# The fourth batch's attention beside the third batch's FFN, and weights narrowed in five operations: attention with sinks and a channel MLP on one core

## The chip, the cores and the metric

The kernel runs on one core of a Trainium2 chip, as one launch. The time is the device time of an execution in microseconds (us). Engines are called TensorE (PE, with its weight loads as PEld), VectorE (DVE), ScalarE (ACT), GpSimd (POOL) and SyncE (SP), whose queue issues nearly all DMAs.

## The reference

```python
scores = scale * np.matmul(q, k.transpose(0, 1, 3, 2))      # 4 batches, 8 heads, S 768, D 64
keep = is_sink | in_window                                  # 4 sink keys, a window of 128
scores = np.where(keep, scores, -1000000000.0)
scores = scores - np.max(scores, axis=-1, keepdims=True)
a = np.exp(scores)
a = a / (np.sum(a, axis=-1, keepdims=True) + 1e-09)
attn = np.matmul(a, v)
...
x = attn.transpose(0, 2, 1, 3).reshape(B, S, H * D)         # 768 x 512 for each batch
xt = x.transpose(0, 2, 1)
h = xt @ U @ V                                              # U 768 x 32, V 32 x 768
u = x + h.transpose(0, 2, 1)
ch = np.maximum(u @ w_ch1, 0.0) @ w_ch2                     # 512 -> 2048 -> 512
return u + ch
```

## The kernel before

Each batch goes through three stages: attention in pairs of heads, the mixing over the sequence (rank 32), and the FFN with its residual. The FFN is most of TensorE's work, so the vector work of one batch's attention is laid beside the FFN of another batch. The table `AHEAD` says which: for the FFN of batch b, the batches that are attended to meanwhile, each with the step at which it begins and a distance:

```python
AHEAD = {0: ((1, 3, 2),), 1: ((2, 0, 1.5), (3, 12, 1.5)), 2: (), 3: ()}
```

All steps are first handed to a planner (class `Plan`), each with its engine or a choice of engines with a cost, what it reads and writes, and a due time. The planner lays them out by its own costs (`order`, with passes backward and forward), tries changes of its due times drawn from numbers that `SEED` and the table `MOVES` fix (`nudge`), and settles for each engine the sequence of its instructions, that of SyncE's DMAs included. Instructions are then issued in that sequence. A change of a cost or of one of these numbers can thus reorder the whole program.

Attention of a pair of heads and half of the rows (`attend`): scores on TensorE (L798), mask and maximum on VectorE (L807, L812), exponentials on ScalarE (L816), the sum plus 1e-9 (L823, on ScalarE or VectorE) and its reciprocal (L826), scaling on ScalarE in three pieces (L834) or GpSimd in one (L837), the copy of the sink columns (L842 to L844), transposes (L857), masked copies `oph` and `opf` (L862, L659), values (L889). K and q are put into two buffers each, `kp` and `qp`, by SyncE's queue (L674), where a load waits until the matmuls of the pair two before have read its buffer.

Mixing: `mix_start` loads the values of the sinks (`vsr`) and splits them into a rounded part and a low part `vsh` (L660, L666, L668), `mix_half` and `mix_end` compute the product with U on TensorE (L1019, L1020), its rounded form `t` (L659 and, for the low part, L1059), the product with V (L1071, L1072) and the sum with x in `xT` (L1074). The function `tt` takes VectorE or GpSimd (L666, L668), `copy` takes ScalarE or VectorE (L659, L660).

Weights, U and V arrive as 64-bit floats. `narrow` turns each piece of up to 512 columns into 32-bit floats on the chip with the steps of `join_steps`: L152 or L153 takes the upper 16 bits, L154 the middle ones, L155 clamps them, L156 or L157 moves the exponent, L158 puts the sign back, L159 (VectorE) or L160 (GpSimd) joins both halves. Weights are then split into a rounded part (cast, L659) and a low part (L666, L668). The one FFN that runs while weights are still arriving is batch 0's (`ffn`): first layer L1109 to L1111 on `uh` and `ul`, the rounded and the low part of u, then `hh` and `hl` (L1117, L1120), and second layer L1131.

Batches 1 to 3 use `ffn_joint`, which forms seven products where eight blocks would be (L1279) from sums of weights `ws` and differences `wd` that lie in DRAM by then; each 256 KB piece is loaded by SyncE's queue and read by six matmuls of 128x384. `combine` forms the sums of u. For batch 2, u lies in DRAM and `combine` reloads it into the buffers `kp` and `qp` (the branch `if b == 2`). This is open to it because `AHEAD` has both batch 2 and batch 3 attended to beside the FFN of batch 1: once that is done, `kp` and `qp` are free. The FFNs of batches 2 and 3 have no attention beside them. After batch 1's FFN, more SBUF is given to weight pieces (`widen`), 13 buffers instead of 7.

## Time and profile before

| | us |
|---|---|
| median of 3 runs | 664.59 |
| the runs | 664.59, 661.3, 665.56 |
| the profiled execution | 662.35 |
| its span | 660.6 |
| TensorE busy | 642.9 |
| VectorE busy | 517.1 |
| ScalarE busy | 436.0 |
| GpSimd busy | 223.1 |

The span runs from the first to the last instruction of the profiled execution. The batches' FFNs follow one another: first matmul of batch 0's at 59.22 us, of batch 1's at 227.97, of batch 2's at 412.01, of batch 3's near 537. Pure matmuls of 128x384 start 0.175 us apart, though each is shown with a length of about 0.33.

### The profile page before, as it was taken

The numbers are of one execution on the slowest core, as the hardware profiler recorded it, in microseconds if no ns is written. First come the engines' busy times: TensorE is split into PE (matmuls) and PEld (weight loads), VectorE is DVE, ScalarE is ACT, GpSimd is POOL, SyncE is SP. The second block draws the span as 40 slices with busy tenths as digits, with TensorE's granted clock in tenths as the row PEclk, the third lists the DMA queues.
The fourth block names the chain that finished last, engine by engine and source line by source line (L and its number), as shares of the span: only waits on it lengthen the run. The fifth ranks groups of instructions, "written<-read, shape, count | busy, mean of one in ns | idle before, by whom it ended". The sixth has DMA issues, their size and how long they took to land.

```text
span 660.6 us, 15908 instructions
## 1 busy us (share of the span) xinstructions
PE 642.9 (97%) x5526; PEld 599.7 (91%) x5526; DVE 517.1 (78%) x1472; ACT 436.0 (66%) x1201; POOL 223.1 (34%) x244
## 2 busy tenths in 40 slices
PE   7899999999999999999999999999999999999996
...
GB/s 254 219 226 382 354 391 350 360 322 352 304 271 336 271 345 377 339 311 215 321 307 360 220 239 287 288 302 250 235 258 247 281 327 342 250 246 247 252 270 92
DMA packets 111721, 191.60 MB, mean 290 GB/s; under 512 B 10256, under 2 KB 46608, under 8 KB 111632
## 3 DMA queue, kind: packets, MB, share of 16 engines
...
q14 instruction: 43, 0.35, 0.2%
...
## 4 chain that ended last, share of the span: by engine, by line
PE 86%; DVE 8%; DMA 3%; issue 1%; POOL 1%; ACT 0%; SPq 0%; DVEq 0%; ACTq 0%; POOLq 0%
PE bank L1279 51%; PE bank L1131 10%; PE bank L798 4%; PE bank L889 4%; PE bank L1109 3%; PE bank L1111 3%; PE bank L1110 3%; PE bank L857 3%; DMA ws<-spare 1%; DVE p L812 1%; DVE w L666 1%; DMA qp<-in_q_dram 1%; DVE spare L666 1%; PE bank L979 1%; DMA kp<-in_k_dram 1%
## 5 line engine op out<-in xcount | busy, mean ns | idle before, releaser
L1279 PE MATMUL bank<-w,w 128*128 128x384 f32 x792 | 155.1, 339 | 0.0
L1279 PEld LDWEIGHTS bank<-w,w 128*128 128x128 f32 x792 | 138.6, 188 | 2.1 <-issue 1.2
L816 ACT ACTIVATE p<-p,mn 128x132 f32<-128x132 f32 x192 | 75.4, 395 | 8.3 <-DVE mn L812 8.1
L1279 PE MATMUL bank<-w,spare 128*128 128x384 f32 x348 | 68.4, 338 | 0.5 <-DVE w L666 0.5
L668 POOL TENSOR_TENSOR spare<-spare 128x128 f32<-128x128 f32 (+1 forms) x56 | 46.2, 837 | 61.6 <-ACT spare L659 13.1
L1284 DVE TENSOR_TENSOR big<-bank,big 128x384 f32<-128x384 f32 x84 | 44.7, 551 | 23.1 <-PE bank L1279 22.8
L1279 PEld LDWEIGHTS bank<-w,spare 128*128 128x128 f32 x348 | 61.6, 188 | 1.0 <-DVE w L666 0.9
L1131 PE MATMUL bank<-w,hh 128*128 128x512 f32 x192 | 61.3, 400 | 0.0
L668 POOL TENSOR_TENSOR w<-uh,w 128x384 fp32r<-128x384 f32 x17 | 17.4, 1021 | 90.9 <-ACT w L659 78.5
L812 DVE CUSTOM_DVE_ANT_0 p<-bank,mask 128x132 f32<-128x132 f32 x192 | 47.5, 291 | 0.2
L659 ACT CAST w<-ul 128x384 fp32r<-128x384 f32 x57 | 29.3, 514 | 23.0 <-PE bank L1279 21.2
L1109 PE MATMUL bank<-ul,w 128*128 128x384 f32 x128 | 43.9, 343 | 0.6 <-POOL ul L668 0.6
L1111 PE MATMUL bank<-uh,w 128*128 128x384 f32 x128 | 43.1, 337 | 0.0
L1110 PE MATMUL bank<-uh,w 128*128 128x384 f32 x128 | 43.0, 336 | 0.0
L1279 PE MATMUL bank<-spare,w 128*128 128x384 f32 x210 | 42.9, 340 | 0.0
L798 PE MATMUL bank<-kp,qp 64*64 64x198 f32 (+3 forms) x840 | 40.7, 325 | 1.4 <-DMA kp<-in_k_dram 1.4
L1131 PEld LDWEIGHTS bank<-w,hh 128*128 128x128 f32 x192 | 34.7, 188 | 6.6 <-issue 1.9
L666 DVE TENSOR_TENSOR w<-ul,w 128x384 fp32r<-128x384 f32 x50 | 30.4, 615 | 10.8 <-ACT w L659 10.4
L1279 PEld LDWEIGHTS bank<-spare,w 128*128 128x128 f32 x210 | 37.0, 188 | 1.4 <-DVE mn L812 0.3
L1131 PE MATMUL bank<-w,hl 128*128 128x512 f32 x96 | 37.9, 395 | 0.0
L834 ACT ACTIVATE p<-p,r 128x132 f32<-128x132 f32 x114 | 36.8, 395 | 0.5 <-DVE r L826 0.5
L798 PEld LDWEIGHTS bank<-kp,qp 64*64 64x64 f32 x840 | 28.9, 139 | 8.6 <-issue 5.3
...
## 6 DMA issues: line engine op xcount, KB each, us to landing
w<-ws SPq DMA_DIRECT2D x132, 256.0 KB, 4.3
w<-wd SPq DMA_DIRECT2D x102, 256.0 KB, 4.2
...
spare<-ws SPq DMA_DIRECT2D x60, 256.0 KB, 3.9
...
spare<-wd SPq DMA_DIRECT2D x42, 256.0 KB, 3.8
...
```

Of the source, the lines that this page charges most:

```text
L666: ways = {"DVE": (dve(n), lambda: nc.vector.tensor_tensor(dst(), a(), b(), op), pool)}
L668: ways["POOL"] = (gps(n), lambda: nc.gpsimd.tensor_tensor(dst(), a(), b(), op), True)
L798: nc.tensor.matmul(st()[a * G:(a + 1) * G, x * TW + to:x * TW + to + wd], qr()[at, q0:q0 + G], kr()[at, k0:k0 + wd], start=True, stop=True ...
L812: add("DVE", dve(SW), lambda st=st, i=i, j=j, at0=x * TW + base + 2 * i, part=part, at=at: nc.vector.tensor_tensor_reduce(part().rearrange ...
L816: add("ACT", act(SW) + 0.22, lambda part=part, at=at: nc.scalar.activation(part(), part(), AF.Exp, bias=at(mn), scale=-1.0, accum_out=at(sm)),
L834: nc.scalar.activation(p()[:, u, i], p()[:, u, i], AF.Copy, scale=r()[:, i * NBLK + u:i * NBLK + u + 1])
L1109: nc.tensor.matmul(ph()[:, :CH], wh, ul()[:, c, :], start=n == 0, stop=False)
L1110: nc.tensor.matmul(ph()[:, :CH], wl, uh()[:, c, :], start=False, stop=False)
L1111: nc.tensor.matmul(ph()[:, :CH], wh, uh()[:, c, :], start=False, stop=n == NC - 1)
L1131: nc.tensor.matmul(acc[k](), a()[:, sl], w()[:, :, at, m:m + P].rearrange("p d o j -> p o d j"), start=not begin and i == 0 and j == 0, st ...
L1279: nc.tensor.matmul(bank()[:, :CH], w()[:, at:at + P], u()[:, d, :] if n > 1 else u(), start=first and i == 1, stop=last and i == 3 * n, sk ...
L1284: add("DVE", dve(CH), lambda: nc.vector.tensor_tensor(x(), bank()[:, :CH], t(), ALU.add), r=(bank,) if t is x else (bank, t), w=(x,), prio ...
```

## The change

The attention of batch 3 is laid beside the FFN of batch 2, and `combine` reads batch 2's sums from the tiles in which they were formed, without the way through DRAM into `kp` and `qp`.

`join_steps` has five steps in place of six. The clamp goes; its lower end is in the shift of the exponent (a Relu of ScalarE with a bias of −8·14336 in a tile `low`, or two instructions of VectorE), its upper end in a minimum of the step that adds (L172). The sign is put in by the last step (L173). Both last steps are VectorE's alone: GpSimd narrows nothing.

GpSimd may take three more kinds of steps: the sink copies and the copies of U into `uf`, and the sum plus 1e-9. The low part of the sinks' values is formed on 32 rows instead of 64, the fourth copy of these values is zero, and the sinks' factor is 1/3 instead of 1/4. For the very first rows of the first pair, the first score step covers one tile of 128 rows and the second two, where it was two and one. The second part of the first k is loaded by ScalarE's queue, behind q; the masks are filled ahead of reading a flag. Costs of the planner for transposes, values and one copy change, and so do SEED and the table MOVES (202 numbers, before 75; cut below).

```diff
@@ -58,25 +58,36 @@
 PRICE = {"DVE": 3.0, "ACT": 1.5, "POOL": 1.5}
-SEED = 510000000
+SEED = 820000000
 SHARES = ((0.02, 6), (0.1, 3), (0.5, 1), (0.005, 15))
...
 MOVES = (
-    14, 17, 59, 72, 119, 122, 174, 241, 268, 327, 385, 575, 576, 601, 647, 662, 670, 673, 700, 759,
...
+    38, 41, 43, 85, 93, 158, 277, 294, 310, 348, 382, 413, 874, 985, 1231, 1234, 1276, 1539, 1665,
...
 )
...
 NEARLY = 1
-VALUES = 2.1
+VALUES = 2.0
 JOINT = (1, 2, 3)
...
 SCRATCH = 1024
-AHEAD = {0: ((1, 3, 2),), 1: ((2, 0, 1.5), (3, 12, 1.5)), 2: (), 3: ()}
+AHEAD = {0: ((1, 3, 2),), 1: ((2, 0, 1.5),), 2: ((3, 0, 1.5),), 3: ()}
 NSLOT = 3
@@ -100,6 +111,7 @@
 TOP_MIN = struct.unpack("f", struct.pack("I", 0x38100000))[0]
+HIGH = float(0x7F80)
 TOP_MAX = struct.unpack("f", struct.pack("I", 0x47EF0000))[0]
@@ -138,7 +150,7 @@
-def join_steps(nc, raw, n, a, t, out):
+def join_steps(nc, raw, n, a, t, out, low):
@@ -146,18 +158,19 @@
     ab = lambda: a().bitcast(BF16)
-    high = lambda: t().bitcast(U16)[:, 1:2 * n:2]
+    high = lambda: f32(t())[:, :n]
     v = nc.vector
+
+    def shifted():
+        v.tensor_scalar(a(), a(), 14336.0, 0.0, ALU.subtract, ALU.max)
+        v.tensor_scalar(high(), a(), 8.0, None, ALU.mult)
     return [
...
         {"ACT": lambda: nc.scalar.activation(x(), mid(), AF.Copy, scale=2.0 ** -13)},
-        {"DVE": lambda: v.tensor_scalar(ab(), ab(), TOP_MIN, TOP_MAX, ALU.max, ALU.min)},
-        {"DVE": lambda: v.tensor_scalar(a(), a(), 14336.0, 8.0, ALU.subtract, ALU.mult),
-          "ACT": lambda: nc.scalar.activation(a(), a(), AF.Copy, bias=-114688.0, scale=8.0)},
-        {"DVE": lambda: v.scalar_tensor_tensor(high(), top(), 0x8000, a(), ALU.bitwise_and, ALU.bitwise_or)},
-        {"DVE": lambda: v.tensor_tensor(x16(), high(), x16(), ALU.add),
-         "POOL": lambda: nc.gpsimd.tensor_tensor(x(), words(t())[:, :n], x(), ALU.add)},
+        {"ACT": lambda: nc.scalar.activation(high(), a(), AF.Relu, bias=low, scale=8.0), "DVE": shifted},
+        {"DVE": lambda: v.scalar_tensor_tensor(x16(), high(), HIGH, x16(), ALU.min, ALU.add)},
+        {"DVE": lambda: v.scalar_tensor_tensor(x16(), top(), 0x8000, x16(), ALU.bitwise_and, ALU.bitwise_or)},
     ]
@@ -653,12 +666,14 @@
-    def copy(self, n, dst, src, psum=False, **kw):
+    def copy(self, n, dst, src, psum=False, pool=False, **kw):
...
         nc = self.nc
-        return self.plan.any({"ACT": (act(n) + (0.0 if psum else 0.045), lambda: nc.scalar.copy(dst(), src()), False),
-                       "DVE": (dve(n) if psum else dve2(n), lambda: nc.vector.tensor_copy(dst(), src()), not psum)},
-                      **kw)
+        ways = {"ACT": (act(n) + (0.0 if psum else 0.045), lambda: nc.scalar.copy(dst(), src()), False),
+                "DVE": (dve(n) if psum else dve2(n), lambda: nc.vector.tensor_copy(dst(), src()), not psum)}
+        if pool:
+            ways["POOL"] = (0.13 + n * 1.1e-3, lambda: nc.gpsimd.tensor_copy(dst(), src()), True)
+        return self.plan.any(ways, **kw)
@@ -688,9 +703,9 @@
         held = (self.held,) if self.raws_seen > NHELD else ()
-        steps = join_steps(self.nc, raw, n, lambda: A()[:, :n], T, flat)
-        use = (((top,), A), ((mid,), flat) if flat else ((), mid), ((), A), ((), A), ((top, A), T), ((T,), flat or mid))
-        cost = (0.069 + n * 0.52e-3, 0.0, 0.069 + n * 0.26e-3, 0.069 + n * 0.26e-3, 0.05 + dve(n), dve(n))
+        steps = join_steps(self.nc, raw, n, lambda: A()[:, :n], T, flat, self.low)
+        use = (((top,), A), ((mid,), flat) if flat else ((), mid), ((A,), T), ((T,), flat or mid), ((top,), flat or mid))
+        cost = (0.069 + n * 0.52e-3, 0.0, 0.138 + n * 0.78e-3, 0.05 + dve(n), 0.05 + dve(n))
         for ways, (r, w), c in zip(steps, use, cost):
@@ -708,9 +723,9 @@
         add("POOL", 0.3, lambda: nc.gpsimd.memset(uf()[:, :, RANK:2 * RANK], 0.0), w=((uf, 1),), prio=pr)
-        self.copy(n, lambda: uf()[:, :, 0:RANK], uv, r=(ub,), w=((uf, 0),), prio=pr)
+        self.copy(n, lambda: uf()[:, :, 0:RANK], uv, pool=True, r=(ub,), w=((uf, 0),), prio=pr)
         self.copy(2 * n, lambda: uf()[:, :, 2 * RANK:].rearrange("p n (a r) -> p n a r", a=2),
-                  lambda: uv().unsqueeze(2).broadcast_to([P, NB, 2, RANK]), r=(ub,), w=((uf, 2),), prio=pr)
+                  lambda: uv().unsqueeze(2).broadcast_to([P, NB, 2, RANK]), pool=True, r=(ub,), w=((uf, 2),), prio=pr)
         for c in range(S // VC):
@@ -821,6 +836,7 @@
         self.plan.any({"ACT": (0.2, lambda: nc.scalar.activation(r(), sm(), AF.Copy, bias=1e-9)),
+                       "POOL": (0.17, lambda: nc.gpsimd.tensor_scalar(r(), sm(), 1e-9, None, ALU.add), True),
                        "DVE": (0.4, lambda: nc.vector.scalar_tensor_tensor(
@@ -855,7 +871,7 @@
                     nc.tensor.transpose(tr()[:, u * P:(u + 1) * P], p().rearrange("p u i w -> p u (i w)")[:, u, at:at + 2 * P - 1:2], self.ident)
-            add("PE", 0.30, mms, r=parts + [box], w=(tr,), prio=t0)
+            add("PE", 0.33, mms, r=parts + [box], w=(tr,), prio=t0)
             banks.append(tr)
@@ -895,12 +911,12 @@
                 src = to if part == 0 else slice(D - to.start, D - to.start + D)
-                self.copy(CH, lambda to=to, cols=cols, xT=xT: xT()[to, cols], lambda src=src, part=part: banks[part]()[src, :CH],
+                self.copy(CH + 85 * part, lambda to=to, cols=cols, xT=xT: xT()[to, cols], lambda src=src, part=part: banks[part]()[src, :CH],
                           psum=True, r=(banks[part],), w=((xT, half),), prio=t0)
...
         row = p, _, sm = self.p(), self.mn(), self.sm()
-        for js in TILES:
+        for js in TILES if b or half or pair else ((0,), (1, 2)):
             self.scores(half, js, t0, q, kr, row)
@@ -939,12 +955,9 @@
-        def vlow(g):
-            sl = slice(g * 32, g * 32 + 32)
-            self.tt(DM, lambda: vs()[sl], lambda: vsr()[sl], lambda: f32(vs()[sl]), ALU.subtract,
-                    r=(vsr,), w=(vs,), prio=t0 - 8)
-        vlow(1)
-        vlow(3)
+        sl = slice(0, 32)
+        self.tt(DM, lambda: vs()[sl], lambda: vsr()[sl], lambda: f32(vs()[sl]), ALU.subtract,
+                r=(vsr,), w=(vs,), prio=t0 - 8)
         self.mixing[b] = vs, None, self.bank
@@ -958,7 +971,7 @@
         self.copy(CH, four, lambda: psink()[:, hs].rearrange("p n h c -> p n (h c)").unsqueeze(2).broadcast_to(
-            [P, NBLK, 4, 32]), r=(psink,), w=(rep,), prio=t0)
+            [P, NBLK, 4, 32]), pool=True, r=(psink,), w=(rep,), prio=t0)
         tr = self.bank()
@@ -1034,7 +1047,7 @@
         part = self.pst(lambda t: f32(t)[:, :P])
-        add("DVE", dve(P), lambda: nc.vector.tensor_scalar(part(), by()[:, :P], 0.25, None, ALU.mult),
+        add("DVE", dve(P), lambda: nc.vector.tensor_scalar(part(), by()[:, :P], 1.0 / 3.0, None, ALU.mult),
             r=(by,), w=(part,), prio=t0)
@@ -1228,13 +1241,6 @@
         xs = self.x[b]
-        if b == 2:
-            us, xs = self.over([((g.boxes[i::NRAW - 1][-1],), lambda g=g, i=i: g.boxes[i::NRAW - 1][-1]()[:, :S])
-                                for g in (self.kp, self.qp) for i in range(NRAW - 1)]), []
-            for d in range(NC):
-                x, ud = us(), self.ud[b][d]
-                self.put(x, lambda x=x, ud=ud: (x(), ud()), 393216, t0, r=(ud,))
-                xs.append(x)
         hi, lo = zip(*[(self.uc(), self.uc()) for _ in range(7)])
@@ -1700,9 +1706,12 @@
                 pre.tile([P, n], F32, name=f"{x}{h}") for x, n in (("kp", NB * SW), ("qp", S))]
-            for part in (slice(0, 2 * SW), slice(2 * SW, NB * SW)):
-                nc.sync.dma_start(kt[:, part], k[0, h][:, part])
-            nc.scalar.dma_start(qt[:, :CH], q[0, h][:, :CH])
+            if h == 0:
+                nc.scalar.dma_start(qt[:, :CH], q[0, h][:, :CH])
+            for x, part in enumerate((slice(0, 2 * SW), slice(2 * SW, NB * SW))):
+                (nc.scalar if h == 0 and x else nc.sync).dma_start(kt[:, part], k[0, h][:, part])
+            if h:
+                nc.scalar.dma_start(qt[:, :CH], q[0, h][:, :CH])
         kept["vp", 0] = pre.tile([P, 2 * NB, D], F32, name="vp0")
@@ -1715,18 +1724,20 @@
         nc.gpsimd.memset(tri, 1.0)
+        low = sp.tile([P, 1], F32, name="low")
+        nc.gpsimd.memset(low, -8.0 * 14336.0)
         for at in (slice(0, G), slice(G, P)):
...
         ns, w, flag = values()
+        masks.fill(ns, w)
         rv = nc.values_load(flag[0:1, 0:1], min_val=0, max_val=1)
-        masks.fill(ns, w)
         nc.gpsimd.memset(join, 0)
...
         with ExitStack() as fctx:
-            Fast(tc, fctx, masks.m, (masks.now, masks.past), tri, ident, kept, pairs, bigs, join,
+            Fast(tc, fctx, masks.m, (masks.now, masks.past), tri, low, ident, kept, pairs, bigs, join,
                  q, k, v, vs, U, V, w1, w2, out).run()
@@ -1763,6 +1774,7 @@
         vs[:, :, h, :, h // 2, h % 2, :] = v[:, None, h, [0, 2, 1, 3] if h % 2 else [2, 0, 3, 1], :]
+    vs[:, 3] = 0.0
     u, vv, w1, w2 = (a["moe_" + n] for n in ("U", "V", "w_ch1", "w_ch2"))
```

What this does to the sequence of instructions is seen at three places.

ScalarE, ahead of the second layer of batch 0's FFN: `uh` are rounded parts of x, `w1_979` (before) and `w1_1073` (after) the first weight of the second layer, `spare0` its narrowed form (of before lines L153, L154, L659; of after L169 to L171, L672). Before:

```order
L659 CAST uh0_1015<-xT1_470 128x384
L659 CAST uh1_1023<-xT1_470 128x384
L153 ACTIVATE nr_1030<-big0_101 128x512
L659 CAST uh1_1023<-xT3_673 128x384
L659 CAST uh1_1023<-xT4_670 128x384
L659 CAST uh1_1023<-xT2_474 128x384
L659 CAST uh0_1015<-xT2_474 128x384
L659 CAST uh0_1015<-xT3_673 128x384
L659 CAST uh0_1015<-xT4_670 128x384
L659 CAST w1_979<-spare0_189 128x4x128
```

After:

```order
L169 ACTIVATE nr_1032<-big2_104 128x512
L672 CAST uh0_989<-xT4_646 128x384
L170 ACTIVATE spare0_191<-big2_104 128x512
L171 ACTIVATE nt_106<-nr_1032,low_127 128x512
L169 ACTIVATE nr_1047<-big3_105 128x512
L170 ACTIVATE spare1_192<-big3_105 128x512
L1130 ACTIVATE hh0_1059<-bank0_183 128x384
L171 ACTIVATE nt_106<-nr_1047,low_127 128x512
L169 ACTIVATE nr_1069<-big0_101 128x512
L672 CAST w1_1073<-spare0_191 128x4x128
L171 ACTIVATE nt_106<-nr_1069,low_127 128x512
L672 CAST w1_1073<-spare0_191 128x4x128
```

The passes over the second half of the first weight (`big2`) stand in the row behind the casts of x that are left, where before both halves had been passed over earlier and only the last cast of this weight is behind them.

VectorE, the same place: the last additions to `xT`, the low parts `ul`, the low part of that weight and the first `hl`. Before:

```order
L1074 TENSOR_TENSOR xT3_673<-xT3_673,bank6_187 128x384
L1074 TENSOR_TENSOR xT4_670<-xT4_670,bank1_182 128x384
L666 TENSOR_TENSOR ul1_1041<-xT2_474,uh1_1023 128x384
L666 TENSOR_TENSOR ul1_1041<-xT4_670,uh1_1023 128x384
L666 TENSOR_TENSOR ul0_1028<-xT2_474,uh0_1015 128x384
L666 TENSOR_TENSOR ul0_1028<-xT3_673,uh0_1015 128x384
L666 TENSOR_TENSOR ul0_1028<-xT4_670,uh0_1015 128x384
L666 TENSOR_TENSOR w1_979<-spare0_189,w1_979 128x4x128
L1120 SCALAR_TENSOR_TENSOR hl0_1092<-bank5_186,hh0_1083 128x384
```

After:

```order
L1087 TENSOR_TENSOR xT4_646<-xT4_646,bank5_188 128x384
L681 TENSOR_TENSOR ul1_1011<-xT3_639,uh1_998 128x384
L681 TENSOR_TENSOR ul0_1000<-xT2_478,uh0_989 128x384
L681 TENSOR_TENSOR ul0_1000<-xT3_639,uh0_989 128x384
L681 TENSOR_TENSOR ul0_1000<-xT4_646,uh0_989 128x384
L172 SCALAR_TENSOR_TENSOR spare0_191<-nt_106,spare0_191 128x512 x2
L173 SCALAR_TENSOR_TENSOR spare0_191<-big1_103,spare0_191 128x512
L173 SCALAR_TENSOR_TENSOR spare0_191<-big2_104,spare0_191 128x512
L1133 SCALAR_TENSOR_TENSOR hl0_1075<-bank0_183,hh0_1059 128x384
L681 TENSOR_TENSOR w1_1073<-spare0_191,w1_1073 128x4x128
```

Four steps of narrowing (L172, L173) now stand between the low parts of x and that of the weight.

SyncE's queue: before, beside the end of batch 1's FFN, with the reloads of batch 2's sums into `kp` and `qp`:

```order
L674 DMA kp0_80<-ud2_0_4815 128x768
L674 DMA qp0_81<-ud2_2_4825 128x768
L674 DMA vp1_831<-in_v_dram 128x768
L674 DMA w3_1190<-wd1_7_1742 128x512
L674 DMA w5_1436<-wd1_5_1246 128x512
L674 DMA w2_1142<-wd1_6_1472 128x512
L674 DMA w3_1190<-wd1_5_1246 128x512
L674 DMA w3_1190<-wd1_4_994 128x512
L674 DMA w4_1304<-wd1_7_1742 128x512
L674 DMA w5_1436<-ws1_4_3207 128x512
L674 DMA kp1_85<-ud2_1_4839 128x768
L674 DMA qp1_86<-ud2_3_4861 128x768
```

After, beside batch 2's FFN, with loads of batch 3:

```order
L689 DMA kp0_80<-in_k_dram 128x792
L689 DMA qp0_81<-in_q_dram 128x768
L689 DMA w3_1180<-wd1_1_2216 128x512
L689 DMA spare1_4692<-ws1_1_2434 128x512
L689 DMA w3_1180<-wd1_0_2018 128x512
L689 DMA w3_1180<-wd1_3_2865 128x512
L689 DMA spare1_4692<-ws1_0_2072 128x512
L689 DMA spare1_4692<-wd1_3_2865 128x512
L689 DMA vp0_95<-in_v_dram 128x768
L689 DMA kp1_85<-in_k_dram 128x792
L689 DMA qp1_86<-in_q_dram 128x768
```

The reloads are gone, and k, q and v of the last two pairs of batch 3 stand among the weights of the next FFN.

## Rows read from the trace of the kernel before

**Rows 1.** The page: busy time by engine, and TensorE's slices of the span in tenths

```profile
PE 642.9 (97%) x5526; PEld 599.7 (91%) x5526; DVE 517.1 (78%) x1472; ACT 436.0 (66%) x1201; POOL 223.1 (34%) x244
PE   7899999999999999999999999999999999999996
```

**Rows 2.** Stretches: length, busy us (count) of PE, PEld, DVE, ACT, POOL; clock, DMA share, GB/s

```profile
0.00:20.00 20.00, 15.24 (x252) 13.73 (x254) 15.53 (x102) 13.95 (x62) 6.56 (x23) 1.00 0.83 279
20.00:40.00 20.00, 15.88 (x332) 12.80 (x322) 19.75 (x91) 19.48 (x80) 10.14 (x16) 1.00 0.49 163
40.00:60.00 20.00, 19.06 (x173) 13.43 (x172) 17.90 (x37) 17.64 (x39) 7.19 (x7) 1.00 0.94 331
60.00:160.00 100.00, 100.00 (x936) 86.79 (x935) 93.14 (x299) 88.55 (x259) 43.43 (x43) 1.00 1.01 361
...
480.00:640.00 160.00, 160.00 (x914) 159.98 (x914) 101.52 (x193) 81.57 (x169) 26.75 (x25) 1.00 0.84 271
```

**Rows 3.** Waits of TensorE: what for, us in total, times, longest

```profile
PE bank L857 <- POOL p L837: 2.7, 3, 1.7
PE bank L857 <- ACT p L834: 2.5, 1, 2.5
PE bank L1020 <- DVE xhl L666: 1.6, 1, 1.6
...
PE bank L1109 <- POOL ul L668: 0.6, 1, 0.6
PE bank L1279 <- DVE w L666: 0.5, 1, 0.5
```

**Rows 4.** Groups by line and shape: busy us, mean ns, idle time before

```profile
L158 DVE SCALAR_TENSOR_TENSOR nt<-big,nr 128x512 uint16<-128x512 uint16 x32 | 25.5, 809 | 0.1
...
L160 POOL TENSOR_TENSOR spare<-nt,spare 128x512 int32<-128x512 int32 x10 | 14.3, 1433 | 21.0 <-DVE nt L158 18.1 <-DVE psink L844 1.4 <-ACT spare L154 0.8
L155 DVE TENSOR_SCALAR nr<-nr 128x512 bf16<-128x512 bf16 x32 | 10.9, 347 | 0.1
...
L823 ACT ACTIVATE r<-sm 128x6 f32<-128x6 f32 x32 | 6.4, 201 | 0.2
```

**Rows 5.** Timeline of the start: begin, us, engine, line, operation [idle before]

```profile
7.67 0.49 DVE L807 COPY_PREDICATED bank<-past,bank 128x128 f32<-128x128 int32 x2 [0.65 <-PE bank L798]
...
21.19 1.27 POOL L668 TENSOR_TENSOR vsh<-xhl,vsh 32x512 fp32r<-32x512 f32 x1 [0.54 <-POOL p L837]
21.28 1.72 DVE L666 TENSOR_TENSOR vsh<-xhl,vsh 32x512 fp32r<-32x512 f32 x1
...
25.36 0.50 PE L857 MATMUL bank<-ident,p 128*128 128x128 f32 x2 [2.50 <-ACT p L834]
```

**Rows 6.** Timeline from t to the second layer, columns as in rows 5

```profile
53.64 0.69 DVE L1059 TENSOR_TENSOR t<-bank,t 32x512 fp32r<-32x512 f32 x1
...
55.81 3.80 DVE L1074 TENSOR_TENSOR xT<-xT,bank 128x384 f32<-128x384 f32 x8
...
57.85 2.62 ACT L659 CAST uh<-xT 128x384 fp32r<-128x384 f32 x6
...
59.53 2.89 DVE L666 TENSOR_TENSOR ul<-xT,uh 128x384 fp32r<-128x384 f32 x5
...
62.34 0.68 DVE L666 TENSOR_TENSOR w<-spare,w 128x512 fp32r<-128x512 f32 x1
...
63.48 0.63 PE L1131 MATMUL bank<-w,hh 128*128 128x512 f32 x2
```

**Rows 7.** The page: DMA issues, KB each, us from issue to landing

```profile
w<-ws SPq DMA_DIRECT2D x132, 256.0 KB, 4.3
```

**Rows 8.** Timeline of TensorE: two score steps of batch 3

```profile
356.70 1.96 PE L798 MATMUL bank<-kp,qp 64*64 64x66 f32 x48
...
370.16 1.96 PE L798 MATMUL bank<-kp,qp 64*64 64x66 f32 x48
```

**Rows 9.** Waits of SyncE's queue: what for, us in total, times, longest

```profile
SPq L674 <- PE bank L798: 23.0, 16, 4.3
```

4 lines of the change are left out of this document (2 added, 2 removed), and 19 rows, old and new, of the table MOVES.

## The prediction

> **What bounds the kernel now.** The page comes first. TensorE is busy 642.9 us of a span of 660.6, and its row of slices shows a low first slice and nines from there to the end [rows 1]. No other engine comes near: VectorE has 78%. So this kernel gets faster only where TensorE waits, or if its work shrinks; it does not shrink here, since the instruction order lists 8,125 TensorE instructions for both programs. The table by stretches tells where the rest sits: in the first 60 us TensorE is busy 15.24 + 15.88 + 19.06 = 50.18 us, so 9.82 us are lost there, and from 60 to 160 us and from 480 to 640 us it is busy throughout [rows 2]. In the second stretch of 20 us VectorE has 19.75 us of work and ScalarE 19.48: there the two vector engines are the bound and TensorE follows. All that comes after runs at TensorE's pace. The waits say which results come late [rows 3]: scaled probabilities (2.7 us in three, 2.5 in one) and, at the mixing of a later batch, a low part of x (1.6); one wait in the last FFNs is 0.5 us. Everything that can be won is therefore some 9.8 us of start and some 2 us in the middle; everything that can be lost is a new wait in the 600 us in which TensorE has none.
>
> **The start, to t.** t is the last small result of batch 0's mixing, and the additions to x, the rounded copies uh and the low parts ul follow it, then FFN 0. I counted the instructions ahead of t's subtraction in the order of each program and priced them by the medians of this trace. On VectorE 56.34 us become 53.91: narrowing of U, V and weights −0.96 (the clamp, 0.35 us for a whole piece [rows 4], goes; the two last steps are both VectorE's now, 0.81 for a whole piece), one subtraction for vs instead of two by VectorE and GpSimd −0.69, one weight's low part that now comes after t −0.69, copies −0.06. ScalarE's sum to the cast of t goes from 47.63 to 43.58, mostly since seven of eight additions of 1e-9 (0.20 each [rows 4]) and three scalings go to GpSimd, which in exchange gives up 5.2 us of narrowing (five additions L160; whole pieces are 1.43 [rows 4]). Two waits go beside this. At 21.28 us VectorE's subtraction of 32 rows took 1.72 us, where such a subtraction takes 0.68 undisturbed [rows 5, 6], while GpSimd worked on the other 32 rows for 1.27 us; the chain behind it ends in the transposes at 25.36, which waited 2.50 us. One of the pair is gone: −1.03. And VectorE's first use of scores waited 0.65 us for all of the first two tiles [rows 5]; the split lets it begin after one. So t comes 2.43 + 1.03 + 0.65 = 4.1 us earlier and ends at 50.2 instead of 53.64 + 0.69 = 54.33 [rows 6].
>
> Here the Trainium skill bears on the row: "SBUF — State Buffer", section "Who interferes with whom", says that a VectorE instruction with two inputs in SBUF contends with a GpSimd instruction that reads SBUF. The trace agrees at that one place, 1.72 us beside GpSimd's 1.27 against 0.68. "Perfetto Trace Analysis", section on optimizing Scalar and DVE operations, adds that moving work between those two "might not help". By that rule the small copies and additions now given to GpSimd would give part of the 1.03 us back; since GpSimd's total to this point falls from about 21 us to about 19, I leave the sum as it is.
>
> **The start, from t to the second layer.** What is earlier at t need not reach TensorE, because the next gate is another: the first second-layer matmul (L1131) needs a weight that is narrowed and split, and h. In the trace it starts at 63.48, 9.15 us after t ended at 54.33, and nothing waits: additions to x 3.80 us, five low parts 2.89, the weight's low part 0.68, ending at 63.02, and hl after it [rows 6]. In the changed order this weight is not as far along. ScalarE's first pass over its second half (L169) stands behind the casts of x (2.62 us for six [rows 6]), and behind that L170, L171, another piece's passes and the cast; on VectorE both L172, both L173 and the low part follow the low parts of x. Laid out by hand from t with this trace's pitches (additions 0.47, low parts 0.55 to 0.58, passes 0.56 to 0.67, two-operand steps 0.65 to 0.8): the last addition ends at 5.15, L169 starts at 5.35, L171 at 7.45, the second cast ends at 11.75, the low part at 12.6, and the matmul starts at 12.85 after t instead of 9.15. TensorE's 32 first-layer steps end near 9.6, so it waits there some 3.3 us. Counted otherwise: VectorE's work to that low part is 65.47 us before and 65.67 after, and ScalarE's to the cast 55.71 and 55.96. The work put off behind t eats what t gained. Gate after: 54.33 − 4.1 + 12.85 = 63.1 against 63.48: **−0.4 us**. Bounds: +1.3, if neither of the two waits that I let go is saved (1.68 of the 4.1), and −4.7, if TensorE need not wait at that gate (4.1, and the 0.6 us for ul behind a GpSimd narrowing step [rows 3]).
>
> **Order of the DMAs, fill of the masks, 1e-9 on GpSimd.** The first scores still wait for the first part of k0, which stays first in its queue; the second part moves behind q0 on the other queue and is wanted later. Zero. The masks' fill is off TensorE's path as well, unless VectorE's first use is at once limited by it: it has 0.65 us there.
>
> **Batch 3's attention moved by one FFN.** TensorE does the same instructions elsewhere. Beside FFN 1, VectorE and ScalarE have room, and beside FFN 2 and 3 more: VectorE is busy 101.5 of 160 us from 480 to 640, ScalarE 81.6 [rows 2]. The load of vector work there is no risk. Four loads of 384 KB fall away on SyncE's queue; six loads of batch 3 (k, q and v of its last two pairs of heads) move from beside FFN 1 to beside FFN 2, among 256 KB weights of which each feeds six matmuls that start 0.175 us apart (1.05 us). The mixing chain of batch 3 moves too; the existing one cost 1.6 us [rows 3]. With the waits of 2.1 us gone or as many new ones coming I take half: **−1.0 us**. Bounds −2.1 (all gone) and +3.2 (two more of the size seen, 1.6).
>
> **Sum.** 662.35 us is the profiled execution's own time, 660.6 of it span. 662.35 − 0.4 − 1.0 = 661. The runs of before have a median of 664.59 and reach from 661.3 to 665.56, so the profile is 2.2 below the median; halfway between both, 663.5 − 1.4 gives **662**. About 1% (6.6 us) is what a measurement of this kernel tells from no change.
>
> **Rivals.** (a) The whole start gain arrives. If ScalarE gets the weight's passes in between the casts, or h comes late anyway, then −4.7 and −2.1 add up: 663.5 − 6.8 = 656.7, on the edge of 1%. For it: 9.8 us of idle time at the start, most of it in waits for the engines that the change relieves. Against: the sums of work to the gate, which do not fall. 0.24. (b) Slower: weights of FFN 2 late. A load of k or q that waits in SyncE's queue for its buffer holds all weights behind it. It decides when a wait exceeds what is in stock: 13 weight buffers × 1.05 = 13.6 us, less 4.3 for a landing [rows 7], 9.3 us. Scores of batch 3 came 13.5 us apart [rows 8]; a load that waits from one to the next costs 13.5 − 9.3 = 4.2 us, and for both pairs 8.4: 663.5 + 4.2 to 8.4, so 668 to 672. Against: such waits of the queue were 23.0 us in 16 [rows 9], 1.4 us at the mean, and TensorE missed no weight. 0.07. (c) t is not earlier. ScalarE is as loaded as VectorE from 20 to 40 us, and if it sets the pace, or GpSimd's small additions arrive late, t stays at 54.33 and the longer way behind it remains: 54.33 + 12.85 − 63.48 = +3.7, giving 666 to 667. 0.12, within 1%. (d) Only the order differs, nothing arrives: 663.5. Within the forecast.
>
> **How the numbers follow.** Forecast with (d) 0.57, (a) 0.24, (b) 0.07, (c) 0.12. Faster by over 1% is under 658: (a), 0.24. Slower by over 1% is over 671: of (b) its upper end, and as much again for a loss in the 600 us without waits that I have not thought of, 0.07 in all. Same: 0.69. The range reaches from 655.5 (a, with 1 us more) to 667 (c); what lies outside is (b) and half of what could go beyond (a).
>
> **What the profile after would show.** t's subtraction ends at about 50 us; the first L1144 at about 63 with TensorE idle about 3 us ahead of it, waiting for a w from VectorE or ScalarE; the wait of 2.5 us at the transposes near 25 us gone; the VectorE subtraction for vs gone; 60 to 655 us without idle time but for 1 us or so at the mixings; last matmul 5 us before the span's end. A first L1144 at 59 makes (a) right; a wait of TensorE for w loaded by DMA beside FFN 2 makes (b) right; t near 54 makes (c) right. A loss spread evenly over the FFNs would come from nothing I have read.

## The result, and the profile after

| | before | after |
|---|---|---|
| median of 19 runs each, us | 662.21 | 667.37 |
| lowest and highest | 660.5, 665.56 | 665.85, 669.04 |
| span of the profiled execution | 660.6 | 666.7 |
| ratio, 95% interval | | 1.007 [1.0059, 1.0081] |

The changed kernel is 5.2 us slower, within the 1% that was called no change but on the other side of the forecast (662.0) and 0.4 us beyond its range. Lines move by 13 to 16: L1144 after is L1131 before, L873 is L857, L813 is L798, L1072 is L1059, L681 is L666, L672 is L659; L169 to L173 are the five steps of narrowing.

The page, busy time and slices, answers to [rows 1]:

```profile
PE 646.0 (97%) x5526; PEld 599.8 (90%) x5526; DVE 520.0 (78%) x1452; ACT 435.1 (65%) x1168; POOL 208.2 (31%) x253
...
PE   6997999999999999999999999999999999999996
...
PEclk9999899999999999999999999999999999999999
```

TensorE has the same 5526 recorded matmuls and is busy 3.1 us longer: it did not only wait, it also ran slower somewhere. The fifth slice (66.7 to 83.3 us) has an 8 in the row of the granted clock. The stretches of the changed kernel (length, busy us of PE, PEld, DVE, ACT and POOL, clock, DMA share, GB/s) answer to [rows 2]:

```profile
0.00:20.00 20.00, 14.66 (x208) 12.41 (x212) 14.79 (x96) 13.54 (x58) 6.99 (x26) 1.00 0.87 299
20.00:40.00 20.00, 18.36 (x378) 14.28 (x371) 18.85 (x95) 19.76 (x78) 12.36 (x22) 1.00 0.56 176
40.00:60.00 20.00, 17.73 (x172) 13.41 (x173) 19.44 (x35) 15.50 (x31) 3.29 (x3) 1.00 0.66 227
...
64.00:66.00 2.00, 0.83 (x2) 0.36 (x2) 0.92 (x2) 2.00 (x4) 1.26 (x1) 0.71 0.93 257
66.00:68.00 2.00, 2.00 (x5) 1.61 (x6) 2.00 (x4) 0.42 (x1) 0.00 (x0) 0.50 1.01 394
68.00:70.00 2.00, 2.00 (x7) 1.52 (x6) 1.48 (x3) 1.16 (x3) 0.27 (x1) 0.50 1.06 365
70.00:72.00 2.00, 2.00 (x7) 1.57 (x6) 0.69 (x1) 1.98 (x4) 1.02 (x1) 0.58 0.86 299
```

From 20 to 40 us TensorE has 18.36 us of work where it had 15.88, so the start did get better there. From 64.8 to 71.7 us it holds half of its full clock, 1.2 GHz (0.71 for 64 to 66 and 0.58 for 70 to 72 give the two ends), where the kernel before held 1.00 from 60 to 160 us [rows 2]. From the gate at 65.10 on it is "busy" in all of that time, which is why the busy share hides it; the counts show it, 5 to 7 matmuls in two us where the kernel before began 11 to 13. One such stretch of the kernel before:

```profile
66.00:68.00 2.00, 2.00 (x11) 1.65 (x10) 2.00 (x5) 2.00 (x5) 0.00 (x0) 1.00 0.92 233
```

TensorE's waits (what for, us, times, longest) answer to [rows 3]:

```profile
PE bank L873 <- POOL p L853: 2.9, 4, 2.0
PE bank L1144 <- ACT w L672: 2.7, 1, 2.7
PE bank L1285 <- DMA w<-wd: 1.7, 3, 1.0
...
PE bank L1085 <- DVE t L1072: 1.0, 1, 1.0
```

The timeline of the changed kernel (begin, us, engine, line, operation, idle before), first of the start and then from narrowing U and V to the second layer, answers to [rows 5, 6]:

```profile
6.15 2.27 PE L813 MATMUL bank<-kp,qp 64*64 64x130 f32 x28 [1.56 <-DVE mask L234]
8.63 3.17 PE L813 MATMUL bank<-kp,qp 64*64 64x130 f32 x56 [0.21 <-DMA qp<-in_q_dram]
13.80 0.98 PE L873 MATMUL bank<-ident,p 128*128 128x128 f32 x6 [1.99 <-POOL p L853]
...
23.66 0.98 PE L873 MATMUL bank<-ident,p 128*128 128x128 f32 x6 [0.40 <-POOL p L853]
...
45.49 1.01 DVE L173 SCALAR_TENSOR_TENSOR big<-big 128x384 uint16<-128x384 uint16 x1
...
50.09 0.73 DVE L173 SCALAR_TENSOR_TENSOR spare<-big,spare 128x512 uint16<-128x512 uint16 x1
...
50.91 0.62 ACT L672 CAST w<-spare 128x512 fp32r<-128x512 f32 x1 [2.35 <-DVE spare L173]
51.43 0.58 ACT L672 CAST t<-bank 128x512 fp32r<-128x512 f32 x1
51.56 0.69 DVE L681 TENSOR_TENSOR w<-spare,w 128x512 fp32r<-128x512 f32 x1 [0.17 <-ACT w L672]
...
52.28 0.69 DVE L1072 TENSOR_TENSOR t<-bank,t 32x512 fp32r<-32x512 f32 x1
53.02 0.44 PE L1085 MATMUL bank<-vst,t 128*128 128x384 f32 x1 [1.04 <-DVE t L1072]
...
60.29 1.40 DVE L172 SCALAR_TENSOR_TENSOR spare<-nt,spare 128x512 uint16<-128x512 f32 x2
61.58 1.35 DVE L173 SCALAR_TENSOR_TENSOR spare<-big,spare 128x512 uint16<-128x512 uint16 x2
...
64.43 0.62 ACT L672 CAST w<-spare 128x512 fp32r<-128x512 f32 x1
...
65.08 0.73 DVE L681 TENSOR_TENSOR w<-spare,w 128x512 fp32r<-128x512 f32 x1 [1.71 <-ACT w L672]
65.10 1.62 PE L1144 MATMUL bank<-w,hh 128*128 128x512 f32 x2 [2.68 <-ACT w L672]
66.95 1.05 PE L1144 MATMUL bank<-w,hh 128*128 128x512 f32 x2
68.23 1.05 PE L1144 MATMUL bank<-w,hh 128*128 128x512 f32 x2
```

t ends at 52.28 + 0.69 = 52.97. The gate of the second layer, the first L1144, comes at 65.10 (63.48 before [rows 6]), after 2.68 us of idle TensorE. Behind it three matmuls take 68.23 − 66.95 = 1.28 us.

To see where the rest lies I priced every recorded TensorE instruction of both traces at the median distance to its successor in the trace before (by source line and shape), and compared the work done by a given time. The changed kernel is 2.5 us ahead at 40 us, 1.2 ahead at 60, 1.6 behind at 65, 4.2 behind at 70 and 4.4 at 80, 3.3 behind at 320, 5.7 at 480 and 6.1 at 640 and at the end. So the loss has two places: the gate with what follows it, and the stretch from 320 to 480 us.

### The profile page after: what moved, and what is told of

The parts are those of the page before. It is cut to its first block, busy times and chain, and to the rows that moved or that the text cites. A ratio compares the mean times of both kernels' runs of the same rounds, so it can differ in the third digit from the quotient of the medians.

```text
span 666.7 us, 15824 instructions
## 1 busy us (share of the span) xinstructions
PE 646.0 (97%) x5526; PEld 599.8 (90%) x5526; DVE 520.0 (78%) x1452; ACT 435.1 (65%) x1168; POOL 208.2 (31%) x253
## 4 chain that ended last, share of the span: by engine, by line
PE 84%; DMA 5%; ACT 5%; DVE 5%; issue 1%; DVEq 0%; SPq 0%; ACTq 0%
PE bank L1285 48%; PE bank L1144 11%; PE bank L813 4%; DMA w<-wd 4%; PE bank L905 4%; PE bank L1122 3%; PE bank L1124 3%; PE bank L1123 3%; PE bank L873 3%; ACT p L831 2%; PE bank L1009 1%; DVE w L681 1%; PE bank L1085 1%; ACT xT L672 1%; PE bank L992 1%
## 5 line engine op out<-in xcount | busy, mean ns | idle before, releaser
L831 ACT ACTIVATE p<-p,mn 128x132 f32<-128x132 f32 x192 | 75.4, 395 | 16.8 <-DVE mn L827 16.1
L1285 PE MATMUL bank<-w,spare 128*128 128x384 f32 x348 | 70.6, 338 | 0.0
L1144 PE MATMUL bank<-w,hh 128*128 128x512 f32 x192 | 63.8, 413 | 2.7 <-ACT w L672 2.7
L683 POOL TENSOR_TENSOR spare<-spare 128x128 f32<-128x128 f32 (+1 forms) x55 | 38.4, 710 | 60.6 <-DVE spare L681 11.9
L672 ACT CAST w<-ul 128x384 fp32r<-128x384 f32 x54 | 27.7, 513 | 31.8 <-PE bank L1285 28.9
L1144 PEld LDWEIGHTS bank<-w,hh 128*128 128x128 f32 x192 | 36.1, 195 | 10.8 <-ACT w L672 3.3
L683 POOL TENSOR_TENSOR w<-uh,w 128x384 fp32r<-128x384 f32 x18 | 19.5, 1081 | 74.0 <-ACT w L672 63.3
L813 PE MATMUL bank<-kp,qp 64*64 64x198 f32 (+3 forms) x840 | 40.7, 323 | 1.8 <-DVE mask L234 1.6
L1144 PE MATMUL bank<-w,hl 128*128 128x512 f32 x96 | 38.9, 405 | 0.0
L681 DVE TENSOR_TENSOR w<-ul,w 128x384 fp32r<-128x384 f32 x49 | 31.2, 639 | 8.4 <-ACT w L672 8.1
L813 PEld LDWEIGHTS bank<-kp,qp 64*64 64x64 f32 x840 | 28.2, 138 | 9.8 <-issue 5.2
L831 ACT ACTIVATION_READ_ACCUMULATOR p<-p,mn 128x1 f32 x192 | 36.2, 189 | 0.0
```

Of the source, the lines that this page charges most:

```text
L672: ways = {"ACT": (act(n) + (0.0 if psum else 0.045), lambda: nc.scalar.copy(dst(), src()), False), "DVE": (dve(n) if psum else dve2(n), la ...
L681: ways = {"DVE": (dve(n), lambda: nc.vector.tensor_tensor(dst(), a(), b(), op), pool)}
L683: ways["POOL"] = (gps(n), lambda: nc.gpsimd.tensor_tensor(dst(), a(), b(), op), True)
L813: nc.tensor.matmul(st()[a * G:(a + 1) * G, x * TW + to:x * TW + to + wd], qr()[at, q0:q0 + G], kr()[at, k0:k0 + wd], start=True, stop=True ...
L831: add("ACT", act(SW) + 0.22, lambda part=part, at=at: nc.scalar.activation(part(), part(), AF.Exp, bias=at(mn), scale=-1.0, accum_out=at(sm)),
L1144: nc.tensor.matmul(acc[k](), a()[:, sl], w()[:, :, at, m:m + P].rearrange("p d o j -> p o d j"), start=not begin and i == 0 and j == 0, st ...
```

## The experiments

Theory A: the wait at the gate lets the clock fall, and the second layer then runs at half clock, which costs some 3 us. Its rival: the clock doesn't matter; what costs is that the gate itself is late. Beside them: D, the order of the first DMAs costs; M, one contended subtraction less buys nothing; and the question what the middle costs.

**Filling the gate's wait.** In the changed kernel, idle matmuls whose results nobody reads are issued ahead of the first L1144.

```diff
+NBANK = 8; GATE, NFILL = 416, 5
...
             for s in order:
+                if s.n == GATE:
+                    rows = self.mask.rearrange("p a b -> p (a b)")[:, :3 * SW]
+                    for _ in range(NFILL):
+                        nc.tensor.matmul(self.banks[3][:, :3 * SW], self.ident, rows, start=True, stop=True)
                 s.fn()
```

> The changed kernel with five extra matmuls of 128x396 (their result is read by nobody) on TensorE in the stretch in which it waits 2.7 us for the first weight of the second layer. Theory A, the fall of the granted clock from 1.00 to 0.50 at 65.1 us follows from TensorE standing idle ahead of it: with the fill the clock stays at 1.00 from 65 to 72 us, the gate stays near 65.1, and the time falls by the 3.2 us that half speed costs there, from 667.4 to about 664.2. Theory B, the clock falls in that stretch whatever TensorE did before (the work that begins there brings it): 0.50 again from 65 to 71 us, and 667.4 or up to 0.3 more.

664.5 us, ratio 1.0034 [1.0021, 1.0047]: 2.9 us less than the changed kernel by the medians, 2.4 by the ratios. Its timeline at the gate (the five matmuls leave ten records) and a stretch behind it:

```profile
62.69 3.49 PE L1529 MATMUL bank<-mask,ident 128*128 128x396 f32 x10
65.71 1.18 PE L1144 MATMUL bank<-w,hh 128*128 128x512 f32 x2
...
66.95 0.63 PE L1144 MATMUL bank<-w,hh 128*128 128x512 f32 x2
...
67.65 0.63 PE L1144 MATMUL bank<-w,hh 128*128 128x512 f32 x2
```

```profile
66.00:68.00 2.00, 1.99 (x9) 1.36 (x8) 2.00 (x5) 0.45 (x1) 0.00 (x0) 1.00 0.97 370
```

The gate opens no earlier (65.71, where it was 65.10), and the kernel still gains: three matmuls now take 67.65 − 66.95 = 0.70 us instead of 1.28. That is theory A; its rival has no way to such a gain. By the measure above (the idle matmuls left out) this profile is level with the changed kernel's at 65 us, 2.3 us ahead at 74 and at 320, and 4.6 ahead at 480. So 2.3 us are won at the gate; the other 2.3 lie between 320 and 480 us, where executions differ by as much without the fill (the fourth step below), and are not shown to be its doing.

**The weight earlier.** Five later narrowing passes of ScalarE are issued behind the casts that the gate waits for, and one step of VectorE ahead of another; `e4_gate_fill` adds two idle matmuls.

```diff
+NBANK = 8; EARLIER = ((383, 392), (453, 414), (454, 414), (455, 414), (463, 414), (465, 414))
...
         order = self.plan.order()
+        step = {s.n: s for s in order}
...
+        for n, ahead in EARLIER:
+            order.remove(step[n])
+            order.insert(order.index(step[ahead]), step[n])
```

> The changed kernel with ScalarE's five narrowing passes over later weights moved behind the first hh and the two casts of the first second-layer weight, and one VectorE step of that weight's first half moved ahead of one of its second half. The cast should end near 63.6 instead of 65.05, so the wait shrinks from 2.7 to about 1.2 us. Theory A (the wait and the clock that falls after it are most of the loss): 1.4 us less if the clock still falls, so 666.0; 4.6 us less, 662.8, if the shorter wait no longer brings the fall. Theory C, the loss is in the FFNs behind it (weights that land late where batch 3's attention has left): the clock and the gate hardly matter, and the time stays within 1 us of 667.4.

> The moved passes of the run before and two of the extra matmuls in what is left of the wait. Theory A: no fall of the clock, gate near 63.6, 4.6 us less than the changed kernel: 662.8, level with the kernel before (662.2). Theory C: within 1 us of 667.4.

665.3 us (1.0039 [1.0021, 1.0056]) and 664.3 (1.0032 [1.0016, 1.0048]). Without a fall at the gate theory A expected 662.8 of both, and it missed by 2.5 and 1.5 us. The first half held: the gate opens at 64.82 and 64.91 after 1.60 us and 0.25 us of idle time, and the clock there is 1.00. But both profiles had another fall, 0.50 at 7 to 14 and 7 to 17 us, behind the first scores. The runs of `e2_gate` spread from 662.41 to 668.56; that such falls spread them is likely and not shown. Filling or shortening the same wait gives the same; the two together add little.

**The same wait, made in the kernel before.** Its last cast of the first second-layer weight is done nine times.

```diff
+NBANK = 8; REPEAT = {402: 9}
...
             for s in order:
-                s.fn()
+                for _ in range(REPEAT.get(s.n, 1)):
+                    s.fn()
```

> The kernel before, with ScalarE's last cast of the first second-layer weight done nine times instead of once (the same values each time), so that the first second-layer matmul comes near 66.0 instead of 63.48 and TensorE waits about 2.5 us there. Theory A (idle TensorE brings the fall of the clock): the granted clock falls to 0.50 for about 6 us in this kernel too, and the time rises by 2.5 + 3.2, from 662.2 to about 667.9. Theory B (the fall belongs to the changed program): clock 1.00 throughout, 2.5 us more, 664.7.

668.7 us, 1.0106 [1.0077, 1.0134], 6.3 us more. TensorE waits 4.10 us at the gate, and then, in the timeline and the stretches:

```profile
68.76 1.22 PE L1131 MATMUL bank<-w,hh 128*128 128x512 f32 x2 [4.10 <-ACT hh L1117]
```

```profile
20.00:40.00 20.00, 16.03 (x322) 12.86 (x314) 19.17 (x85) 18.44 (x78) 9.93 (x15) 0.91 0.43 143
...
70.00:72.00 2.00, 2.00 (x6) 1.52 (x6) 2.00 (x5) 0.75 (x2) 0.00 (x0) 0.50 0.19 65
```

The kernel before loses its full clock in the same way once it waits at the same place. The price of the fall is not separated here: the gate opens 68.76 − 63.48 = 5.28 us later than before, more than the wait, in an execution with another fall (0.91 from 20 to 40 us), and 6.3 us is 1 us more than that delay.

**The first DMAs as before**, in the changed kernel: q0 behind k0, both parts of k0 on SyncE's queue.

```diff
-            if h == 0:
-                nc.scalar.dma_start(qt[:, :CH], q[0, h][:, :CH])
-            for x, part in enumerate((slice(0, 2 * SW), slice(2 * SW, NB * SW))):
-                (nc.scalar if h == 0 and x else nc.sync).dma_start(kt[:, part], k[0, h][:, part])
-            if h:
-                nc.scalar.dma_start(qt[:, :CH], q[0, h][:, :CH])
+            for part in (slice(0, 2 * SW), slice(2 * SW, NB * SW)):
+                nc.sync.dma_start(kt[:, part], k[0, h][:, part])
+            nc.scalar.dma_start(qt[:, :CH], q[0, h][:, :CH])
```

> The changed kernel with the first DMAs as before: both parts of the first k on SyncE's queue, three q in a row on ScalarE's. In the changed kernel TensorE's first transposes start at 13.80 us (13.03 before), since the scores of the second and third tile wait for q behind the second part of k and the parameters land 0.2 us later. Theory D (the new order of DMAs costs at the start): scores of the three tiles without a gap, first transposes near 13.1, 0.7 to 1.4 us less than the changed kernel, so 666.0 to 666.7. Theory E (the prediction's zero: what is late there is made up for by slack of VectorE): the transposes may come earlier, the time stays at 667.4 within 0.4.

665.91 us, 1.0041 [1.0024, 1.0059]: 1.5 us less than the changed kernel by the medians, 1.9 by the ratios (the two intervals just touch). Its start in the timeline:

```profile
6.05 4.95 PE L813 MATMUL bank<-kp,qp 64*64 64x130 f32 x84 [1.48 <-DVE mask L234]
13.00 0.99 PE L873 MATMUL bank<-ident,p 128*128 128x128 f32 x6 [2.00 <-POOL p L853]
```

The scores run as one block again and the first transposes come 0.80 us earlier; t's low part starts at 51.52 instead of 52.28 and the gate opens at 64.34 instead of 65.10, after the same 2.68 us of idle time. So 0.76 us of the gain is seen there; the rest is not located.

**Both, and t ahead of the weights.** `e5_dma` with the moves of `e2_gate`, t's cast and low part issued ahead of a weight's, and two first-layer low parts given to GpSimd. Then the same with two idle matmuls at the gate and one more round of idle matmuls at the very start (`NSPIN` 9).

```diff
+NBANK = 8; ONPOOL = (365, 375); EARLIER = ((383, 392), ... (374, 379), (375, 379))
...
+        for n in ONPOOL:
+            step[n].fn = step[n].ways['POOL'][1]
...
-NSPIN = 8
+NSPIN = 9
```

> The first DMAs as before, the moved passes of the run e2_gate, and t ahead: ScalarE's cast of t and VectorE's low part of t stand before the cast and the low part of a first-layer weight, whose two low parts go to GpSimd, idle there for 15 us. Theory A with D: t ends 1.2 us earlier than in e2_gate, the gate comes at 62 to 63, the clock stays at 1.00, and the sum of e2_gate (665.3), 1.2 for t and 0.7 to 1.4 for the start gives 662.7 to 663.4, level with the kernel before. Theory F (GpSimd beside VectorE eats it, or what is late next is the weight): gate at 64 or later, 665.

> The run e6_early with two of the extra matmuls in what is left of TensorE's wait ahead of the second layer, and nine start-up matmuls instead of eight, so that TensorE stands idle a shorter time ahead of the first scores. In e6_early the granted clock was 0.50 from 8 to 10.5 us, in e5_dma from 64 to 71 us, in others elsewhere. Theory A (idle stretches bring a fall of the clock, in some executions and not in others): fewer falls, 0.5 to 1.5 us less than e6_early's 664.1, so 662.6 to 663.6. Theory B (the falls have nothing to do with what TensorE did before): 664.1 within 0.4.

664.13 us (1.0014 [0.9999, 1.003]) and 663.69 (1.0037 [1.0023, 1.0051], beside 661.51 of the kernel before in that session). In `e6_early` t's low part starts at 50.40 and the gate opens at 62.10, 3.0 us earlier than in the changed kernel and 1.4 earlier than before; the time is still not under that of the kernel before, and 0.7 us above the forecast; its profile has a fall at 7.5 to 10.9 us. `e9_level` had no fall at the gate but one at 12 to 16 us, which the last experiments take up. Its 663.69 lies between its two theories and, by the ratios, is no better than `e6_early`: it decides nothing.

**Without the tuned moves.** Both kernels with the table MOVES empty, and of the changed one also with the six-step narrowing, and with the old AHEAD and its reload.

```diff
-MOVES = (
-    38, 41, 43, 85, 93, ...
-)
+MOVES = ()
```

> The changed kernel with an empty table of MOVES, so that its order is the planner's own. Theory G (the 202 numbers are worth several us, and what they bring is not lost in the start): slower than the changed kernel by over 3 us, above 670. Theory H (the order that the numbers reach is no better on the chip than the planner's own, since the planner doesn't see the fall of the clock): 664 to 670.

> The kernel before with an empty table of MOVES. Against e7_plain_after it compares the change without numbers on either side. Theory G: its 75 numbers bring several us, above 666, and the plain changed kernel may even be the faster of the two. Theory H: within 3 us of 662.4, and below e7_plain_after, as the tuned ones are.

> The run e7_plain_after (the changed kernel without numbers, 673.7) with the six narrowing steps of before. The prediction's count gives the five steps an advantage of VectorE of some 1 us up to t and nothing at the gate. Theory I (the new steps are dearer than counted, 1.05 instead of 0.79 us on 384 columns, and ScalarE's pass with the bias 0.72 instead of 0.63): 2 to 4 us less, near e8_plain_before's 667.7. Theory J (narrowing makes no difference that an order without numbers would not blur): 671 to 676.

> The run e7_plain_after (673.7) with batch 3's attention back beside batch 1's FFN and the reload of batch 2's sums. Theory C (the move costs, since weights of batch 1's FFN land late once that attention no longer spreads their use): the stretch from 80 us to the end gets 1.5 to 3 us shorter, 671 to 672. Theory K (the move changes nothing): 673.7 within 1.5, with the difference in the first 80 us.

673.69 (1.0163 [1.0128, 1.0197]), 667.7 (1.0071 [1.0045, 1.0096]), 666.11 (1.0055 [1.0033, 1.0077]) and 665.75 (1.0067 [1.0044, 1.0089]). Going back on either part alone wins 7.6 or 7.9 us, more than all that separates the two plain kernels (6.0); so these are not the prices of the parts. The profiles say what else differs: 0.50 at 8 to 18, 38 to 42 and 69 to 73 us in the plain changed kernel, 9 to 12 with six steps, 43 to 47 with the old AHEAD, 13 to 17 and 68 to 71 in the plain kernel before. Each edit reorders the whole start, and with it the waits that drop the clock; that this decides is argued and not shown. This test doesn't tell narrowing from AHEAD.

**One subtraction instead of two, in the kernel before**, with the zero copy and the factor 1/3 that go with it. The other subtraction keeps its place in the plan and is not issued.

```diff
-            sl = slice(g * 32, g * 32 + 32)
+            sl = slice(0, 32)
...
-        vlow(1)
+        vlow(1); SKIP.add(self.plan.steps[-1].n)
         vlow(3)
...
-        add("DVE", dve(P), lambda: nc.vector.tensor_scalar(part(), by()[:, :P], 0.25, None, ALU.mult),
+        add("DVE", dve(P), lambda: nc.vector.tensor_scalar(part(), by()[:, :P], 1.0 / 3.0, None, ALU.mult),
...
-                s.fn()
+                if s.n not in SKIP:
+                    s.fn()
...
+    vs[:, 3] = 0.0
```

> The kernel before with one part of the change and its own order: one subtraction of 32 rows on GpSimd for the sinks' values (the other left out, the fourth copy zero, factor 1/3). VectorE's 1.72 us at 21.28 go, and TensorE's wait of 2.5 us at the transposes at 25.36 shrinks to about 1. Theory L (what is late there is passed on to the second layer's start, which has no slack in this kernel): 1.0 to 1.7 us less than before, 660.6 to 661.3. Theory M (VectorE's work between there and the gate sets the end, and the gate's weight is no earlier): 662.3 within 0.4.

662.24 us, 1.0004 [0.9993, 1.0016]. The wait at the transposes near 25 us falls from 2.50 [rows 5] to 1.49, and nothing is won in the time, as theory M had it. M's reason is not shown: in the execution that was profiled the clock fell twice, and the gate came at 65.05, later than the 63.48 of the kernel before:

```profile
12.00:16.00 4.00, 2.91 (x30) 2.44 (x34) 2.88 (x20) 3.71 (x18) 1.17 (x3) 0.65 0.93 332
26.00:30.00 4.00, 4.00 (x47) 2.89 (x51) 3.35 (x17) 3.21 (x15) 2.54 (x5) 0.61 0.25 79
```

**Filling the start's waits.** Idle matmuls, into the bank that the transposes take next: in the kernel before three ahead of the first transposes and four ahead of those near 25 us; in `e9_level` four ahead of the first.

```diff
+NBANK = 8; START, GATE, NFILL, SKIP = {59: 3, 156: 4}, -1, 0, ()
...
             for s in order:
+                rows = self.mask.rearrange("p a b -> p (a b)")[:, :3 * SW]
+                for _ in range(START.get(s.n, 0)):
+                    nc.tensor.matmul(self.banks[s.takes[0].slot][:, :3 * SW], self.ident, rows, start=True, stop=True)
...
```

> The kernel before with idle matmuls (128x396, results overwritten) issued where TensorE waits in the start: three ahead of the first transposes (13.0 us), four ahead of those at 25.4 us. The output is unchanged. Theory G (what differs from one execution to the next, and 1 us or more of the median, are stretches in which the granted clock falls to 0.50 after these waits): the stretches at 13 to 16 and 26 to 30 us stay at 1.00 and the median is 0.5 to 1.5 us under the kernel before, ratio 0.998 to 0.9995. Theory H (the start hangs on VectorE and ScalarE, and a fall there is hidden behind their work): no change, within 0.3 us, or some tenths slower for the matmuls added.

> The kernel of e9_level with four idle matmuls ahead of the first transposes. Theory G: no clock under 0.9 between 7 and 75 us, and the median falls by 1 us or so under that of e9_level (663.69 beside 661.51 of the kernel before, ratio 1.0037): ratio 1.001 to 1.0025. Theory H: ratio 1.003 to 1.0045 as e9_level.

The kernel before falls to 661.14 us, 0.998 [0.9969, 0.999], faster than both kernels; the changed one comes to 662.51, 1.0001 [0.9985, 1.0017]. The stretches of `e13_start_before`, against those of `e12_one_sub` above:

```profile
12.00:16.00 4.00, 3.32 (x38) 2.09 (x36) 3.65 (x26) 4.00 (x19) 1.74 (x3) 1.00 0.92 297
26.00:30.00 4.00, 4.00 (x123) 3.41 (x121) 3.97 (x18) 4.00 (x19) 2.25 (x4) 1.00 0.30 96
```

And of `e9_level`, then of `e14_start_after`:

```profile
12.00:15.00 3.00, 2.44 (x22) 2.05 (x26) 1.84 (x11) 3.00 (x15) 1.16 (x4) 0.56 0.96 340
```

```profile
12.00:15.00 3.00, 3.00 (x23) 2.03 (x24) 2.14 (x19) 3.00 (x14) 1.28 (x3) 1.00 0.97 353
```

The mean granted clock of each run agrees: the 29 runs of the kernel before in that session lie between 0.992 and 0.999, median 0.996, the 12 of `e13_start_before` between 0.995 and 1.0, median 0.999. So the kernel before, whose profiled execution shows 1.00 from the start to 658 us, has such falls in most of its runs. What one costs differs: in all 104 of its runs that were taken along with the experiments, the 14 with a mean clock of 0.998 or more have a median of 661.4 us and the 11 with 0.993 or less one of 663.3, but the 79 between reach from 660.67 to 666.18. Theory G held in both kernels. For the changed one the gain is 2.3 us against the kernel before, from `e9_level` to `e14_start_after`, where 1 was expected; the intervals allow both.

**Without the fourth batch's late loads.** `e1_fill` with the six loads of k, q and v beside the third FFN left out.

```diff
+NBANK = 8; START, GATE, NFILL, SKIP = {}, 416, 5, (3212, 3213, 3214, 3275, 3276, 3277)
...
-                s.fn()
+                if s.n not in SKIP:
+                    s.fn()
```

> The kernel of e1_fill with the six loads of k, q and v of the fourth batch's last two pairs of heads, beside the third batch's FFN, left out: the fourth batch's attention then reads what is left in the buffers, so its result is not the reference's. If these loads among the weights are what costs in the middle: 1 to 1.5 us under e1_fill, ratio 1.0010 to 1.002 where e1_fill had 1.0034. If the middle's loss comes from the second batch's FFN, from whose later part the attention was taken, or from the mixing: no change, 1.003 to 1.004.

664.31 us, 1.0022 [1.0008, 1.0036], against 1.0034 [1.0021, 1.0047] of `e1_fill`: it lies between the two forecasts, the intervals overlap, and the work lost from 320 to 480 us by the measure above is 16.5 us here, 16.1 there. So these loads are not shown to cost anything. TensorE's waits for weights stay (its waits from 320 to 480 us):

```profile
PE bank L1285 <- DMA w<-wd: 0.8, 1, 0.8
PE bank L1285 <- DMA w<-ws: 0.4, 1, 0.4
```

## Why the prediction was wrong

**The base.** Three runs (median 664.59) were weighed with the profile to 663.5; 19 runs have 662.21. That is 1.3 us too much, and it flattered the forecast by luck: the predicted difference was −1.4, the measured one +5.2.

**What held.** The bound was read rightly: TensorE follows the vector engines in the start and is alone afterwards. The transposes' wait of 2.50 us went (now 0.40, at 23.66), VectorE's subtraction for vs went, the gate waits for a w, 2.68 us of idle time where 3.3 was foreseen, and the way from t to the gate grew to 65.10 − 52.97 = 12.13 us, where 12.85 was laid out. From 480 us on the loss grew by only 0.4 us.

**First failed step: t 4.1 us earlier.** It came 54.33 − 52.97 = 1.36 us earlier, 2.74 less than foreseen; the shorter way to the gate gave 0.72 back, so the gate is 1.62 us later than before instead of 0.4 earlier. The stretches up to t, before and after:

```profile
0.00:54.33 54.33, 45.14 (x717) 35.53 (x717) 47.63 (x216) 46.17 (x168) 19.82 (x40) 1.00 0.72 243
```

```profile
0.00:52.97 52.97, 44.19 (x717) 34.46 (x717) 46.16 (x209) 43.40 (x154) 19.35 (x47) 1.00 0.66 225
```

VectorE's busy time fell by 47.63 − 46.16 = 1.47 us. The prediction had 2.43 + 1.03 = 3.46 for it, since the 1.03 was part of the 1.72 us of one subtraction; and its idle time, from which 0.65 was to go, rose from 6.70 to 6.81. The counted 56.34 us could also not have fitted into the 53.64 us ahead of t's subtraction: in the trace instructions of VectorE overlap (their lengths add up to 61.95 us, 47.63 busy), so what leaves such a sum is worth less than its length. Three more reasons stand in rows. The joining steps of U and V write back into the 64-bit words that they read: 1.01 us at 45.49 for 384 columns, more than the 0.81 that I took for a whole piece of 512, and than the 0.73 that such a piece takes into the flat `spare` (50.09). ScalarE's cast of t stood in line behind a cast of a weight that waited 2.35 us for VectorE (50.91). And VectorE did two low parts of weights (the second at 51.56) ahead of that of t. `e6_early`, with t's cast and low part in front of them, has t's low part 1.12 us earlier than `e5_dma`. I counted work ahead of t, engine by engine, and not who waits for whom in those queues.

**Second: "the first scores still wait for k0 ... Zero".** They started at 6.15, much as before (5.95), though the row puts that start down to VectorE's mask step (L234), which the prediction had off TensorE's path; but the second part waited for q at 8.63 and the first transposes came at 13.80 instead of 13.03. `e5_dma` prices the order of the first DMAs at 1.5 us. It lies partly in the first step too, as the 0.76 us by which t moves there.

**Third, and the largest: a term that was not in the sum.** I foresaw TensorE idle for 3.3 us and priced the wait alone. The 2.68 us wait was followed by some 6.5 us of matmuls at half clock, about 3.2 us of lost work; `e1_fill` gets 2.9 back (2.4 by the ratios) without opening the gate earlier, and `e3_late` brings the fall into the kernel before. The Trainium skill, "TensorE: Matmul & The Clock Gate", section "HAM oscillation — how this bites in real kernels", says that a TensorE held up by a DMA wait between bursts of matmuls is throttled and begins the next burst at half rate. The trace agrees, 0.50 from 66 to 70 us behind 2.68 us of idle time, though that section treats waits for DMAs that recur in a loop, and here it is one wait, for ScalarE's cast.

**Fourth: −1.0 for the move of batch 3's attention.** The wait of 1.6 us [rows 3] went, as said. But by the measure above (160 us less the priced work; only differences count), eleven profiles with the new AHEAD lose 15.8 to 18.6 us from 320 to 480 us, mean about 17, and six with the old one 15.2 to 16.0, mean 15.6: about +1.4. The spread is wide: the changed kernel has 18.6, `e5_dma` with the same fall at the gate 16.0, and five of the eleven lie at 16.1 or below. In all eleven TensorE waits there for weights from DRAM, 0.6 to 1.7 us; in none of the six. The place is mostly the later part of batch 1's FFN, which lost the attention that spread its matmuls; of the changed kernel's 1.7 us, 0.49 come at 398.02, in batch 2's FFN, which begins at 389.53. Its stretch in the changed kernel, and one of the kernel before up to the end of that FFN:

```profile
320.00:389.00 69.00, 67.66 (x378) 65.51 (x377) 53.84 (x110) 40.18 (x82) 19.84 (x18) 1.00 0.97 331
```

```profile
320.00:412.00 92.00, 90.42 (x998) 85.41 (x996) 80.84 (x258) 66.17 (x214) 44.57 (x45) 1.00 0.86 283
```

The DMA engines go from 0.86 to 0.97 of their time. That the waits follow from this share is argued and not tested on its own, and the share alone does not part the profiles: from 320 to 389 us both `e10_plain_six`, which waits 0.8 us for a weight, and `e8_plain_before`, which waits for none, have 0.92. The rest of the +1.4 stays open: `e13_start_before` and `e14_start_after`, both filled, still differ by 662.51 − 661.14 = 1.4 us, but they differ in narrowing as well.

**The rivals.** (a) fell: its mark was a gate at 59 us. (b), weights late by the queue of k and q, did not come: weights were late, but not shown to be by those loads (`e15_noload`), and mostly in the other FFN; its mark, a wait for a weight beside batch 2's, came as 0.49 us only. (c) foresaw +3.7 at the gate with t at 54.33; it was +1.6 with t at 52.97. Its total of 666 to 667 is nearest to the measured one, by another cause.

**The account.** In the profiles, the gate is 1.6 us late, the half clock costs 2.3 more up to 74 us, and the middle 1.4 in the mean: 5.3, with 5.2 measured. By edits, 2.9 us (fill at the gate) and 1.5 (DMAs) of 5.2 have been taken back one by one; all repairs together, with the start's waits filled, bring the changed kernel level with the kernel before, 1.0001 [0.9985, 1.0017]. Level is not better: against the kernel before with its own start filled nothing remains of the change's gain.
